# Weight loads issued by GpSimd, the second weight split in place, and the order planned anew

## The chip, the core and the metric

The kernel runs on one core of a Trainium2 chip. Its engines are TensorE (PE, with the weight load PEld beside it), VectorE (DVE), ScalarE (ACT), GpSimd (POOL) and SyncE (SP), which here only issues DMAs. Each engine works through its own queue in order, and semaphores tie the queues together. DMAs can be issued from SP, ACT and POOL. The metric is the device time in microseconds from launch to the last store; a profile of one execution stands beside the timed runs.

## The reference

Block-sparse attention feeds an MLP with the mish activation. The weights come as float64, everything else as float32.

```python
# attention: batch 4, heads 8, seq 768, head_dim 64, blocks of 32, 3 random blocks a row of blocks
scores = scale * np.matmul(q, k.transpose(0, 1, 3, 2))
mask = np.abs(blk_i - blk_j) <= 1            # the window
mask = mask | (blk_i == 0) | (blk_j == 0) | (blk_i == 23) | (blk_j == 23)   # the global blocks
...                                          # and the sampled blocks of each row
attn = softmax(np.where(mask, scores, -1e9))
x = (attn @ v).transpose(0, 2, 1, 3).reshape(3072, 512)
# MLP
h = x @ w_in                                 # 512 x 2048
g = h * np.tanh(softplus(h))
return (g @ w_out).astype(np.float32)        # 2048 x 512
```

## The kernel before

**Arithmetic.** Every matmul operand that must be exact is split in a high and a low float16 half, and three products (high-high, high-low, low-high) make one product. So each weight block goes through: a load of the float64 bits (1024 KB for one of the 8 blocks of w_in, 512 KB for one of the 16 of w_out), a decode to float32 on DVE in three integer operations (L873, L876, L879), a sum of squares on PE (the "gram", L361) from which a power-of-two scale comes, and the split in two halves. For w_in the split runs over PE (L947, L956) and casts on ACT or DVE (L951, L953). For w_out, `add_split` with `by_pe` false (`OPE` is 0) does it in three steps: scale the float32 into a temporary wt_o (ACT L963 or DVE L965), cast that to the high half (ACT L968 or DVE L969), and subtract on POOL to get the low half (L970). The decoded float32 block of w_out lies in the very bytes of wo that its two halves take later (`a0_o`).

**Attention.** The queries are worked on in jobs, 13 for each of four batches: first a dense one for the first global block, then pairs of query blocks, with the other dense one in between. A job makes the scores s (L661), their maximum (L703 to L708, DVE), the exponentials pt (L727, ACT), transposes t (L667, PE), the two halves ph (L750, ACT) and pl (L754, DVE; in the first three jobs PE L758 and ACT L763), the product with v (L789, into obank), the division (L808 to L811, DVE), a transpose tx and its halves xh (L836) and xl (L839). Keys of the random blocks are gathered by POOL copies (L598, or on ACT L595 in the first jobs), values by DMAs that SP issues (L615 to L622 for a pair, L637 for a dense job, L558 for the global blocks) from a copy vd in DRAM.

**MLP.** A tile is 256 tokens. Its h (L1049) comes in 8 parts; each pair of parts goes through scale (L1060), exponentials and logarithms (L1078 to L1086), L1087 and the halves g (L1094 or L1096, and POOL L1099); then y (L1114) takes four k steps for each half of the tile, which need the halves of w_out. The ring g has four places, so the h of the next tile can run ahead of the y of the tile before by no more than that.

**Order.** Nothing is scheduled by the compiler. Each step is a task with its engines, a duration in us and what it reads and writes. `Plan.emit` runs a model of the engines and, at each step, picks for the engine that is free first the task with the smallest sum of due time and key; the instructions are then written in that order. The keys stand in tables: `URGE` by kind of task, `JOBS` by job (the first 14), `PIECES` by weight block. `START` gives the earliest time at which PE may begin the scores of each of the first 14 jobs, and `pace` spreads the others. `fill` puts matmuls that do no work (L1309) into gaps of PE from 14 to 200 us. In the model a DMA takes its queue's time; it knows nothing of the semaphores that mark completion.

**Rings.** Buffers are handed out from rings of fixed length (`RINGS`). The ring "raw" has 6 places; it holds the loaded k, q and v of coming batches (L419), the v halves, the raw blocks of w_out, and the temporaries wt_o. The ring "wr" of raw w_in blocks has 3. `load_i` and `load_o` issue the weight loads, on ACT or, where the model finds it earlier (`BOTH`), on SP. All of them record line L865, in `load_w`.

The three steps of a w_out block before:

```python
nc.vector.tensor_scalar(out=t, in0=a0(), scalar1=sc(), scalar2=None, op0=ALU.mult)      # or ACT
nc.vector.tensor_copy(out=hi, in_=tl[kt])                                               # or ACT
nc.gpsimd.tensor_tensor(out=lo, in0=tl[kt], in1=hi, op=ALU.subtract)
```

Of the kernel before, what the change touches and what calls it, by code (L numbers as in the profile page):

```python
# [32 lines left out]
URGE = {"am": -30, "dgi": -29, "endsv": 24, "gh": 8, "gp": -3, "gram": 4, "gramv": 1, "hik": -7, "hiq": 20, "hiv": -7, "hs": 4, "hsw": -16, "k": -4, "kg": -1, "kw": -30, "mx": 19, "nb": -12, "o": 13, "p": -1, "ph": 2, "pl": -30, "q": 12, "r": 30, "rawk": 6, "rawq": 23, "rawv": 24, "s": -10, "sck": 12, "scq": -24, "scv": -3, "ssk": -22, "ssq": 1, "ssv": 9, "t": 14, "tpq": -30, "tpv": 2, "tpw": -12, "tx": -30, "us": -2, "v": -1, "vd": -9, "vg": 1, "wdi": -4, "whi": -3, "who": -30, "wli": -27, "wlo": -11, "wo": 19, "wor": 24, "wq": 7, "wr": -23, "ws": 1, "wto": 26, "xhw": 22, "xw": 10, "ys": -7}  # L33
JOBS = [-17, -8, 5, -19, 0, 1, -8, -9, -24, -11, 1, 1, -4, -26]
PIECES = [-4, -2, -1, 2, -1, 3, 5, 18, -23, -12, -10, -4, -3, -4, 3, 8, 7, 11, 13, 14, 16, 23, 31, 26]
# [29 lines left out]
class Plan:  # L65
# [4 lines left out]
    SEM = 0.06  # L70
# [53 lines left out]
    def emit(self, pace, fill):  # L124
# [6 lines left out]
        free, ready, dma, held = {}, {}, {}, {}  # L131

# [9 lines left out]
        while todo:  # L142
# [3 lines left out]
            for eng, ts in ready.items():  # L146
                f = free.get(eng, 0.0)
                cand = []
                for t in ts:
# [10 lines left out]
                    if len(t.ways) > 1:  # L160
                        done = {e: max(at, load.get(e, 0.0)) + x[0] for e, x in t.ways.items()}
                        if done[eng] > min(done.values()):
                            continue
                    start = self.port(held, eng, max(at, f), t.ways[eng][2])
# [17 lines left out]
            if t.kind and t.kind[0] == "dma":  # L182

                other = max([x for e, x in dma.items() if e != t.eng], default=0.0)
                at = max(dma.get(t.eng, 0.0), end)
                dma[t.eng] = at + t.kind[1] + min(t.kind[1], 0.5 * max(other - at, 0.0))
                t.end = max(dma[t.eng], end + t.lat)
# [21 lines left out]
def attn_mish_kernel(ctx: ExitStack, tc: tile.TileContext, qT, kT, v, sampled, blocks, w_in, w_out, out):  # L209
# [118 lines left out]
    BOTH = True  # L328
# [70 lines left out]
    def add_root(key, ss, fn, r, after, w, new, cls, n=1, apart=False, ring="t"):  # L399

        add("PE", 0.3 * n, lambda: root_pe(key, ss(), apart, ring), r=r, w=[key], new=[(ring, key)], key=cls - 2, lat=0.3)
        add("DVE", 0.6, fn, r=[key, *after], w=w, new=new, key=cls)

    def load(b, what, js, ring="raw", after=()):
# [3 lines left out]
        def fn():  # L408
# [15 lines left out]
            kind=("dma", 1.95 * n))  # L424
# [114 lines left out]
    def store_v(b, j):  # L539
        add("SP", 0.9, lambda: nc.sync.dma_start(  # L540
            out=vd[b][j * TT:(j + 1) * TT].rearrange("(c p) h d -> p c h d", p=P), in_=tl["v", b, j]),
            r=[("v", b, j)], w=[("vd", b, j)], key=-4, lat=2.5, kind=("dma", 2.0))
# [12 lines left out]
    def globals_v(b, n):  # L555
# [3 lines left out]
        add("SP", 0.9, fn, r=VD3(b), w=[("vg", n)], key=-1, lat=2.3, kind=("dma", 0.5))  # L559
# [46 lines left out]
    def gather_v(su):  # L606
# [6 lines left out]
        def fn():  # L613
# [10 lines left out]
            kind=("dma", 0.9))  # L624
# [733 lines left out]
```

## Time and profile before

| | |
|---|---|
| timed runs | 788.79, 789.8 and 790.77 us |
| median | 789.8 us |
| the profiled execution, first to last instruction | 786.6 us, mean granted clock 0.990 |
| h matmuls (L1049), PE busy | 282.8 + 209.8 us |
| y matmuls (L1114), PE busy | 278.0 us |
| weight loads: first and last issue of w_in | 10.5 and 50.9 us |
| weight loads: first and last issue of w_out | 60.4 and 105.3 us |
| first matmul of h, first of y | 102.6 and 143.0 us |
| bytes moved by DMA | 95.31 MB, on SP's queue 80.51 MB, on ACT's 12.85 MB |

The profiled execution's time is given as its span; 3.2 us lie between that and the median of the timed runs. Busy times of PE overlap, because matmuls are pipelined. A row of a group ends with the idle time of its engine just ahead of the group's instructions and with what ended it. A row of waits names who waited, for whom, how long in all, how often, and the longest. A row of a stage gives its length and the busy time of each engine in it. A row of a tile gives the shortest, the median and the longest duration in ns, and the first and last start.

### The profile page before, as it was taken

What the parts mean: (1) busy time and instruction counts of PE and PEld (TensorE: products, weight loads), DVE (VectorE), ACT (ScalarE), POOL (GpSimd) and SP (SyncE); (2) the same over time, 40 slices, a digit from 0 to 9 for tenths busy, and PEclk for the clock granted to TensorE, in tenths of its full rate; (3) what the DMA queues carried; (4) which work ended last, traced back from release to release, by engine and by line L of the source; (5) the groups of instructions that cost most, each with busy time, mean ns of one, the idle gap of its engine ahead of it and who ended that gap; (6) DMA issues with size and microseconds to landing.
All of it is one profiled execution on the core that took longest, in us unless ns stands there. A gap on an engine that the chain in (4) does not pass through costs nothing.

```text
span 786.6 us, 30628 instructions
## 1 busy us (share of the span) xinstructions
PE 740.5 (94%) x12793; PEld 518.7 (66%) x12793; DVE 493.5 (63%) x900; ACT 542.7 (69%) x880; POOL 307.6 (39%) x393
## 2 busy tenths in 40 slices
PE   6677899888999999999999999999999999999997
PEld 5544578665577767767776676677677667666663
DVE  6868988998767764795866457656665453223220
ACT  3555778768868877777887768786876666455650
POOL 2114244887635542374443422534641331213021
PEclk9989999999999999999999999999999999999999
DMA  9878857104534475244346603523444112000000
GB/s 339 263 236 256 268 176 202 44 2 136 159 117 131 119 198 171 69 162 120 87 139 194 192 15 101 174 77 91 119 115 119 37 39 81 14 15 14 14 14 27
DMA packets 57742, 95.31 MB, mean 121 GB/s; under 512 B 8323, under 2 KB 20612, under 8 KB 57604
## 3 DMA queue, kind: packets, MB, share of 16 engines
q1 hardware_dynamic: 52032, 80.51, 34.9%
q10 hardware_dynamic: 5572, 12.85, 4.8%
q8 instruction: 100, 1.64, 0.9%
q14 instruction: 38, 0.31, 0.1%
HBM read 80.38 MB, written 12.95 MB: 119 GB/s over the span
## 4 chain that ended last, share of the span: by engine, by line
PE 73%; DVE 10%; ACT 6%; DMA 5%; issue 2%; POOL 1%; SPq 1%; POOLq 1%; ACTq 0%; DVEq 0%
PE h_None L1049 27%; PE y L1114 26%; PE obank L789 6%; PE t L667 6%; PE s L661 4%; DMA vg<-vd 3%; PE tx L667 1%; PE wd_i L947 1%; DVE wt_o L965 1%; DMA wr<-in_moe_w_in_dram 1%; DVE hs_None L1087 1%; DVE v L491 1%; DMA raw_k<-in_k_dram 1%; ACT us_None L1078 1%; POOL kt L522 1%
## 5 line engine op out<-in xcount | busy, mean ns | idle before, releaser
L1049 PE MATMUL h_None<-xh,wi 128*128 128x256 f16 x1536 | 282.8, 273 | 0.0
L1114 PE MATMUL y<-wo,g 128*128 128x512 f16 x1152 | 278.0, 380 | 4.0 <-POOL wo L970 2.6
L1049 PEld LDWEIGHTS <-wi 128*128 128x128 f16 x2304 | 223.5, 98 | 47.3 <-issue 2.1
L1049 PE MATMUL h_None<-xl,wi 128*128 128x256 f16 x768 | 209.8, 273 | 0.0
L1114 PEld LDWEIGHTS <-g 128*128 128x128 f16 x1152 | 111.1, 98 | 106.7 <-issue 7.3
L1099 POOL TENSOR_TENSOR g<-hs_None,g 128x1024 f16<-128x1024 f32 x48 | 107.6, 2241 | 188.4 <-DVE g L1096 144.8
L598 POOL COPY kg<-kt 128x256 f16 x258 | 107.2, 451 | 123.3 <-PE s L661 109.7
L1060 ACT ACTIVATE hs_None<-h_None,gsc 128x512 f32<-128x512 f32 x96 | 65.5, 684 | 80.2 <-PE h_None L1049 79.4
L727 ACT ACTIVATE pt<-s,nb,ns 128x256 f32<-128x256 f32 (+1 forms) x208 | 106.3, 582 | 5.7 <-PE t L667 5.0
L750 ACT ACTIVATE ph<-t 128x512 f16<-128x512 f32 x112 | 66.5, 596 | 45.1 <-PE t L667 45.0
L754 DVE SCALAR_TENSOR_TENSOR pl<-t,ph 128x512 f16<-128x512 f32 x105 | 71.9, 686 | 35.8 <-ACT ph L750 35.5
L1087 DVE SCALAR_TENSOR_TENSOR hs_None<-us_None,hs_None 128x1024 f32<-128x1024 f32 x48 | 65.0, 1355 | 40.1 <-ACT us_None L1086 40.1
L667 PE MATMUL t<-ident,pt 128*128 128x128 f32 x448 | 70.4, 280 | 6.8 <-DVE pl L754 3.6
L708 DVE TENSOR_REDUCE mx<-s 128x4 f32<-128x1024 f32 x44 | 53.7, 1222 | 31.9 <-PE s L661 31.3
L1083 POOL TENSOR_TENSOR us_None<-us_None 128x1024 f32<-128x1024 f32 x22 | 44.2, 2007 | 71.8 <-DVE us_None L1081 68.7
L667 PEld LDWEIGHTS t<-ident,pt 128*128 128x128 f32 x448 | 51.6, 142 | 21.4 <-DVE pl L754 4.5
L789 PEld LDWEIGHTS <-ph 128*32 128x32 f16 x3584 | 47.9, 94 | 20.9 <-issue 13.1
L1078 ACT ACTIVATE us_None<-hs_None,hsc 128x1024 f32<-128x1024 f32 x48 | 55.2, 1150 | 0.9
L789 PE MATMUL obank<-vg,ph 128*32 128x65 f16 (+1 forms) x3200 | 50.6, 196 | 4.0 <-DMA vg<-vd 2.2
L1081 DVE TENSOR_SCALAR us_None<-us_None 128x1024 f32<-128x1024 f32 x48 | 37.4, 778 | 25.4 <-ACT us_None L1078 25.2
L1085 ACT ACTIVATE us_None<-us_None 128x1024 f32<-128x1024 f32 x48 | 50.7, 1056 | 1.6 <-POOL us_None L1083 0.8
L1086 ACT ACTIVATE us_None<-us_None 128x1024 f32<-128x1024 f32 x48 | 50.7, 1056 | 0.8
(199 smaller groups left out, 893.6 us busy)
## 6 DMA issues: line engine op xcount, KB each, us to landing
vg<-vd SPq DMA_DIRECT2D x320, 65.0 KB, 2.6
vg<-vd SPq DMA_DIRECT2D x80, 195.0 KB, 3.2
wr<-in_moe_w_in_dram ACTq DMA_DIRECT2D x8, 1024.0 KB, 7.4
vd<-v SPq DMA_DIRECT2D x12, 520.0 KB, 3.8
vg<-vd SPq DMA_DIRECT2D x12, 520.0 KB, 5.1
raw_k<-in_k_dram SPq DMA_DIRECT2D x12, 512.0 KB, 5.4
raw_q<-in_q_dram SPq DMA_DIRECT2D x12, 512.0 KB, 4.3
raw_v<-in_v_dram SPq DMA_DIRECT2D x12, 512.0 KB, 5.0
```

Of the source, the lines that this page charges most:

```text
L598: nc.gpsimd.tensor_copy(out=dst, in_=tl["kt", b][:, :, ds(j, BS)])
L667: nc.tensor.matmul(out, src, ident, start=start, stop=stop, is_transpose=True)
L727: ex = lambda o, x, g, w: nc.scalar.activation(out=o, in_=x, func=AF.Exp, bias=nb[:, g, w:w + 1], scale=tl["ns", b, sus[w]["qb"] // TB][:, ...
L750: nc.scalar.activation(out=new(sb, "ph", ("ph", i, j), [P, 2, 2, P], F16), in_=tl["t", i, j], func=AF.Copy, scale=PSC)
L754: nc.vector.scalar_tensor_tensor(out=new(sb, "pl", ("pl", i, j), [P, 2, 2, P], F16), in0=tl["t", i, j], scalar=PSC, in1=tl["ph", i, j], op ...
L789: nc.tensor.matmul(o[cs, w, g, 0:v1 - v0], p[:, k, g, cs], vt[:, k, 2 * c + g, v0:v1], start=j == 0 and g == 0 and k == 0 and n == 0, stop ...
L1049: nc.tensor.matmul(h[:, f2, 0:n].rearrange("p (s q) -> p s q", q=BS), wi[:, fp, cc // 2, w, cc % 2, fs], x[:, s0:s0 + sn, cc], start=f2 == ...
L1060: nc.scalar.activation(out=tl[kq][:, 2 * (fp % 2):2 * (fp % 2) + 2, 0:n], in_=tl[kh][:, :, 0:n], func=AF.Copy, scale=gsc[:, fp:fp + 1])
L1078: nc.scalar.activation(out=us(), in_=hs(), func=AF.Exp, scale=hsc[:, b:b + 1])
L1087: add("DVE", 1.32 * c, lambda: nc.vector.scalar_tensor_tensor(out=hs(), in0=us(), scalar=-0.5, in1=hs(), op0=ALU.add, op1=ALU.mult), r=[ku ...
L1099: add("POOL", 2.3 * c, lambda: nc.gpsimd.tensor_tensor(out=g(1), in0=hs(), in1=g(0), op=ALU.subtract), r=[kq, ("gh",) + kp], w=[kp], use=[kg])
L1114: nc.tensor.matmul(tl[ky], tl["g", b, t, k][:, g, f, q], wo[:, fc, w], start=fc == 0 and n == 0, stop=fc == NFC - 1 and n == 2)
```

## The change

The loads of both weights are issued by GpSimd alone, no longer by ACT or SP. A block of w_out is split in two operations and without a temporary: the high half is scaled straight out of the float32 block, on ACT or DVE, and DVE makes the low half in one operation (scale, then subtract the high half). The halves of block n are written where the float32 of block n - 2 was, which is free once that block's own halves are made; the halves of the first two go to a new buffer wx. In the planner, a DMA now takes the next of eight semaphores of its kind of queue (one set of eight for SP and ACT, one for POOL) and starts only when that semaphore's last DMA has landed; a task that issues several DMAs counts each, and the times of some are new. The first matmuls of h wait for the scale gsc in the plan, too, and the small matmul of a scale waits for what its DVE step waits for. The tables `URGE`, `JOBS`, `PIECES` and `START` have new numbers throughout; the earliest starts of the 14 first jobs are shown below.

```diff
...
-    SEM = 0.06
+    SEM, LANES = 0.06, 8
     def __init__(self, rings):
...
         free, ready, dma, held = {}, {}, {}, {}
+        lanes = {w: [[0.0] * self.LANES, 0] for w in ("hard", "soft")}
         def open_(t):
...
                             continue
+                    if t.kind and t.kind[0] == "dma":
+                        lane, n = lanes["soft" if eng == "POOL" else "hard"]
+                        at = max(at, lane[n % self.LANES])
                     start = self.port(held, eng, max(at, f), t.ways[eng][2])
...
             if t.kind and t.kind[0] == "dma":
-                other = max([x for e, x in dma.items() if e != t.eng], default=0.0)
-                at = max(dma.get(t.eng, 0.0), end)
-                dma[t.eng] = at + t.kind[1] + min(t.kind[1], 0.5 * max(other - at, 0.0))
-                t.end = max(dma[t.eng], end + t.lat)
+                lane, n, end, t.end = *lanes["soft" if t.eng == "POOL" else "hard"], start, 0.0
+                each = t.kind[1] / t.kind[2]
+                for k in range(n, n + t.kind[2]):
+                    end = max(end, lane[k % self.LANES]) + t.dur / t.kind[2]
+                    other = max([x for e, x in dma.items() if e != t.eng], default=0.0)
+                    at = max(dma.get(t.eng, 0.0), end + 0.3)
+                    dma[t.eng] = at + each + min(each, 0.5 * max(other - at, 0.0))
+                    lane[k % self.LANES] = land = max(dma[t.eng] + 0.5, end + t.lat + min(max(other - end, 0.0), 3.5))
+                    t.end = max(t.end, land)
+                lanes["soft" if t.eng == "POOL" else "hard"][1] += t.kind[2]
+                free[t.eng] = end
             else:
...
     NO, NZ = 4 * (D + 2), 240
-    BOTH = True
     pools = {"w": ctx.enter_context(tc.tile_pool(name="never", bufs=1))}
...
     def add_root(key, ss, fn, r, after, w, new, cls, n=1, apart=False, ring="t"):
-        add("PE", 0.3 * n, lambda: root_pe(key, ss(), apart, ring), r=r, w=[key], new=[(ring, key)], key=cls - 2, lat=0.3)
+        add("PE", 0.3 * n, lambda: root_pe(key, ss(), apart, ring), r=[*r, *after], w=[key], new=[(ring, key)], key=cls - 2, lat=0.3)
         add("DVE", 0.6, fn, r=[key, *after], w=w, new=new, key=cls)
...
             new=[(ring, key) for key in keys], key=-5 if b == 0 else 0, lat=2.0,
-            kind=("dma", 1.95 * n))
+            kind=("dma", 1.45 * n, n))
     def sums(b, what, j, cls):
...
             out=vd[b][j * TT:(j + 1) * TT].rearrange("(c p) h d -> p c h d", p=P), in_=tl["v", b, j]),
-            r=[("v", b, j)], w=[("vd", b, j)], key=-4, lat=2.5, kind=("dma", 2.0))
+            r=[("v", b, j)], w=[("vd", b, j)], key=-4, lat=2.5, kind=("dma", 2.0, 1))
     KT3 = lambda b: [("k", b, j) for j in T3]
...
                 nc.sync.dma_start(out=vgs[n][s * BS:(s + 1) * BS, 1], in_=vd[b][j * BS:(j + 1) * BS])
-        add("SP", 0.9, fn, r=VD3(b), w=[("vg", n)], key=-1, lat=2.3, kind=("dma", 0.5))
+        add("SP", 0.9, fn, r=VD3(b), w=[("vg", n)], key=-1, lat=2.3, kind=("dma", 0.5, 2))
     regs = {}
...
         add("SP", 2.9, fn, r=VD3(b) + ["off", "z"] + [("reg", k) for k, _ in slots(su)], w=[("vg", n)], key=-3, lat=2.4,
-            kind=("dma", 0.9))
+            kind=("dma", 1.5, 2 + NR - 1 + (w0 - qb != -1 or w1 - qb != 2)))
     def fetch_dense(su):
...
                 w=[("vg", j) if j < NVG else ("vt", b)], new=[("raw", ("vt", b))] if j >= NVG else (),
-                key=-3, lat=2.4, kind=("dma", 2.0))
+                key=-3, lat=2.4, kind=("dma", 2.0, 1))
...
             go = lambda eng: load_w(pools["w"], raw, "wr", src, None, eng)
-            add("ACT", 0.45, lambda: go(nc.scalar), r=after, w=[raw], new=[("wr", raw)], key=-9, lat=2.0,
-                kind=("dma", 3.9), also=[("SP", 0.5, lambda: go(nc.sync), False)] if BOTH else ())
+            add("POOL", 1.0, lambda: go(nc.gpsimd), r=after, w=[raw], new=[("wr", raw)], key=-9, lat=2.0,
+                kind=("dma", 3.9, 1))
             return
-        add("ACT", 0.45, lambda: load_w(None, None, None, src, a0_i(k).rearrange("p (c f) -> p c f", c=NCC),
-                                          nc.scalar), r=after,
-            w=[key], key=-9, lat=2.0, kind=("dma", 1.95))
+        add("POOL", 1.0, lambda: load_w(None, None, None, src, a0_i(k).rearrange("p (c f) -> p c f", c=NCC),
+                                        nc.gpsimd), r=after,
+            w=[key], key=-9, lat=2.0, kind=("dma", 1.95, 1))
     def piece_i(k, cls):
...
             also=[("DVE", 0.68, lambda: cast("DVE", lo), False)])
+    SH = 2
+
+    def wo_at(fc):
+
+        return pools["wx"][:, fc] if fc < SH else wo[:, fc - SH]
+
     def a0_o(fc):
         go = lambda eng: load_w(sb, raw, "raw", w_out.rearrange("(c p) f -> p c f", p=P)[:, fc], a0_o(fc), eng)
-        add("ACT", 0.45, lambda: go(nc.scalar), r=after, w=[raw] + ([] if wide else [("wo", fc)]), new=[("raw", raw)],
-            key=-5, lat=2.0, kind=("dma", 1.95), also=[("SP", 0.5, lambda: go(nc.sync), False)] if BOTH else ())
+        add("POOL", 1.0, lambda: go(nc.gpsimd), r=after, w=[raw] + ([] if wide else [("wo", fc)]), new=[("raw", raw)],
+            key=-5, lat=2.0, kind=("dma", 1.95, 1))
     def piece_o(fc, cls):
...
     def parts_o(fc, cls):
-        if fc == 0:
-            add_diag(("o",), lambda: sc_o, "sc_o", cls)
-        add_split(("o", fc), ("o",), lambda: a0_o(fc), wo[:, fc, 0], wo[:, fc, 1], ("wo", fc), RINGO, cls,
-                  lambda: sc_o, "sc_o", fc % 4 < OPE)
+
+        before = [(w, "o", fc - SH) for w in ("wh", "wl")] if fc >= SH else ["open"]
+        kh, kl = ("wh", "o", fc), ("wl", "o", fc)
+
+        def hi(eng):
+            if eng == "ACT":
+                nc.scalar.activation(out=wo_at(fc)[:, 0], in_=a0_o(fc), func=AF.Copy, scale=sc_o)
+            else:
+                nc.vector.tensor_scalar(out=wo_at(fc)[:, 0], in0=a0_o(fc), scalar1=sc_o, scalar2=None, op0=ALU.mult)
+        add("ACT", 0.62, lambda: hi("ACT"), r=[("wo", fc), "sc_o", *before], w=[kh], key=cls,
+            also=[("DVE", 0.45, lambda: hi("DVE"), True)])
+        add("DVE", 0.72, lambda: nc.vector.scalar_tensor_tensor(
+            out=wo_at(fc)[:, 1], in0=a0_o(fc), scalar=sc_o, in1=wo_at(fc)[:, 0], op0=ALU.mult, op1=ALU.subtract),
+            port=True, r=[("wo", fc), "sc_o", kh], w=[kl], key=cls)
     def scales_w():
...
         for f2 in range(2):
-            mlp(1.31 if part is None else 0.85, lambda f2=f2: fn(f2), r=[*PARTS_I(fp), *xs], w=[kh, "h in order"],
+            mlp(1.31 if part is None else 0.85, lambda f2=f2: fn(f2), r=[*PARTS_I(fp), "gsc", *xs], w=[kh, "h in order"],
                 new=[("h", kh)] if f2 == 0 else (), use=[("xh", b, t), ("xl", b, t)])
...
                 for n, (g, w) in enumerate(((0, 0), (0, 1), (1, 0))):
-                    nc.tensor.matmul(tl[ky], tl["g", b, t, k][:, g, f, q], wo[:, fc, w],
+                    nc.tensor.matmul(tl[ky], tl["g", b, t, k][:, g, f, q], wo_at(fc)[:, w],
                                      start=fc == 0 and n == 0, stop=fc == NFC - 1 and n == 2)
...
                 also=[("ACT", 0.7, lambda: ys_fn("ACT"), False)])
-            add("SP", 0.4, out_fn, r=[kys], lat=2.0, kind=("dma", 1.1))
+            add("SP", 0.4, out_fn, r=[kys], lat=2.0, kind=("dma", 1.1, 1))
...
         pools["m"] = pools["cm"].__enter__()
+        pools["wx"] = pools["m"].tile([P, SH, 2, DM], F16, name="wx", tag="wx", bufs=1)
     LPE = 4
-    OPE = 0
-    RINGO = "t"
     AT0, ATV, ATW = -19.0, -13.0, -4.0
...
     add("ACT", 1.0, lambda: which(new), w=["off", "z"],
-        new=[("hs", ("z",))], key=-9, lat=6.0)
+        new=[("hs", ("z",))], key=-9, lat=6.0, kind=("dma", 0.9, 2 + B))
     for j in T3:
...
     total = sum(t.ways["PE"][0] for t in plan.tasks if t.kind and t.kind[0] == "M")
-    RES, START = 595.0, [0, 58, 39, 56, 33, 120, 63, 62, 76, 58, 107, 143, 72, 148]
+    RES, START = 595.0, [9, 54, 61, 56, 37, 142, 59, 75, 33, 90, 112, 155, 52, 144]
     at = {"done": 0.0, "next": 0.0, "job": 0, "last": None, "shape": None, "open": False}
...
```

`add_decode`, the gram and the split of w_in stay as they are.

More of the change, by code (lines that the diff above doesn't have):

```diff
@@ L28 @@
              wq=2, am=2, dg=2)
-URGE = {"am": -30, "dgi": -29, "endsv": 24, "gh": 8, "gp": -3, "gram": 4, "gramv": 1, "hik": -7, "hiq": 20, "hiv": -7, "hs": 4, "hsw": -16, "k": -4, "kg": -1, "kw": -30, "mx": 19, "nb": -12, "o": 13, "p": -1, "ph": 2, "pl": -30, "q": 12, "r": 30, "rawk": 6, "rawq": 23, "rawv": 24, "s": -10, "sck": 12, "scq": -24, "scv": -3, "ssk": -22, "ssq": 1, "ssv": 9, "t": 14, "tpq": -30, "tpv": 2, "tpw": -12, "tx": -30, "us": -2, "v": -1, "vd": -9, "vg": 1, "wdi": -4, "whi": -3, "who": -30, "wli": -27, "wlo": -11, "wo": 19, "wor": 24, "wq": 7, "wr": -23, "ws": 1, "wto": 26, "xhw": 22, "xw": 10, "ys": -7}
-JOBS = [-17, -8, 5, -19, 0, 1, -8, -9, -24, -11, 1, 1, -4, -26]
-PIECES = [-4, -2, -1, 2, -1, 3, 5, 18, -23, -12, -10, -4, -3, -4, 3, 8, 7, 11, 13, 14, 16, 23, 31, 26]
+URGE = {"am": -11, "dgi": -30, "endsv": 30, "gh": 14, "gp": -24, "gram": 30, "gramk": 30, "gramq": 1, "gramv": -6, "hik": -26, "hiq": -2, "hiv": -22, "hs": -2, "hsw": -7, "k": 23, "kg": 5, "kw": -22, "mx": 28, "nb": -7, "o": 14, "p": 1, "ph": -15, "pl": -20, "q": 3, "r": 30, "rawk": -24, "rawq": 2, "rawv": 30, "s": -9, "sck": 30, "scq": -26, "scv": -6, "ssk": -9, "ssq": 2, "ssv": 2, "t": 29, "tpk": 14, "tpq": -27, "tpv": -6, "tpw": -22, "tx": -20, "us": -5, "v": -30, "vd": -21, "vg": 29, "wdi": 4, "whi": 5, "who": -13, "wli": -21, "wlo": -16, "wo": 19, "wor": 30, "wq": 8, "wr": -24, "wto": 26, "xhw": 16, "xw": -12, "ys": 4}
+JOBS = [-30, -22, 0, -1, 30, 10, -17, -30, -30, -28, -9, 1, -11, -30]
+PIECES = [-3, 0, -6, 2, -1, 14, 20, 30, -6, -26, -8, -2, 5, -19, 16, 5, 9, 17, 11, 13, 1, 12, 29, 30]
 def place(w):
```

## The prediction

> **What bounds the kernel now.** I read the page's head first, then the busy time by stage, then the waits of the two bad stages, and last the tiles that the change touches.
>
> ```profile
> span 786.6 us, 30628 instructions
> PE 740.5 (94%) x12793; PEld 518.7 (66%) x12793; DVE 493.5 (63%) x900; ACT 542.7 (69%) x880; POOL 307.6 (39%) x393
> 0.00:40.00 40.00, 26.55 (x481) 21.88 (x482) 30.38 (x78) 18.24 (x28) 8.15 (x23) 1.00 0.87 298
> 40.00:100.00 60.00, 47.74 (x1077) 29.10 (x1075) 47.51 (x99) 38.83 (x84) 16.37 (x27) 0.91 0.83 257
> 100.00:140.00 40.00, 38.74 (x1044) 32.78 (x1044) 33.69 (x69) 33.31 (x63) 19.32 (x27) 1.00 0.63 180
> 140.00:180.00 40.00, 32.24 (x396) 23.35 (x381) 39.01 (x50) 28.44 (x41) 33.22 (x26) 1.00 0.05 15
> 180.00:200.00 20.00, 20.00 (x293) 12.57 (x292) 16.00 (x27) 17.41 (x31) 15.42 (x18) 0.91 0.53 160
> 200.00:600.00 400.00, 393.91 (x7808) 280.54 (x7807) 268.54 (x498) 307.86 (x518) 176.23 (x251) 1.00 0.44 126
> 600.00:700.00 100.00, 99.52 (x1217) 68.40 (x1216) 39.71 (x62) 58.61 (x81) 21.26 (x15) 1.00 0.17 49
> 700.00:786.60 86.60, 81.79 (x515) 50.09 (x513) 18.70 (x22) 39.98 (x43) 17.66 (x8) 0.99 0.05 19
> ```
>
> The columns of the stages are the length, then the busy time of PE, its weight load, DVE, ACT and POOL, then the granted clock, the DMA share and GB/s. TensorE bounds the kernel from 200 us on: it idles 6.1 us of 400, then 0.5 and 4.8. Before 200 us it idles 13.5, 12.3, 1.3 and 7.8 us (length less busy), and some of its busy time is no work: the filler of L1309.
>
> ```profile
> 0.00:40.00 40.00, 11.23 (x88) 9.18 (x89) 1.00 0.87 298
> 40.00:100.00 60.00, 4.33 (x24) 1.96 (x21) 0.91 0.83 257
> ```
>
> So 15.6 us are filler. The clock of 0.91 costs about 47.74 x 0.09 = 4.3 us in 40:100 and 20.0 x 0.09 = 1.8 us in 180:200. Together, idle 46.1, filler 15.6 and clock 6.1 make 68 us that are not work at full clock. Nothing in the diff changes the matmul work, so a gain can only come out of these 68 us, and nearly all of what the changed operations touch lies before 200 us: 21 us in 40:100 and 9.6 us in 140:200.
>
> In 140:180 DVE is the bound (39.01 of 40) and the DMA engines stand still (share 0.05). Why they do, the waits and the timeline of SP's own queue tell:
>
> ```profile
> SPq L419 <- POOL wo L970: 22.9, 3, 20.3
> SPq L419 <- ACT wo L968: 19.0, 1, 19.0
> 132.41 8.24 SPq L637 DMA_DIRECT2D vg<-vd  x3
> 179.96 3.77 SPq L419 DMA_DIRECT2D raw_v<-in_v_dram  x3
> ```
>
> L419 loads v of the second batch into the ring "raw". It waits 42 us for slots that the temporary wt_o of the second weight's split holds. SP issues in order, so nothing leaves it from 140.65 to 179.96 us.
>
> In 40:100 the largest hole is this, from the waits of the first 100 us and the timeline:
>
> ```profile
> ACT wi L951 <- DMA vg<-vd: 6.4, 1, 6.4
> PE wd_i L956 <- ACT wi L951: 5.5, 1, 5.5
> 48.68 0.38 ACTq L865 DMA_DIRECT2D wr<-in_moe_w_in_dram  x1
> ```
>
> ACT's next compute reads nothing of vg. What waited was the weight load at 48.68, which stands ahead of it in ACT's queue, and it was released by the landing of one of SP's gathers. The two share their completion semaphores; that is how I read it. PE stood 5.5 us behind it.
>
> **The change, part by part.**
>
> 1. *24 weight loads go to POOL.* Eight of w_in leave ACT, sixteen of w_out leave ACT and SP, eight each.
>
> ```profile
> L865 ACTq DMA_DIRECT2D wr<-in_moe_w_in_dram x8: 374/374/520, 10.5 to 50.9; - x8
> L865 ACTq DMA_DIRECT2D wor<-in_moe_w_out_dram x8: 334/366/710, 60.4 to 89.3; - x8
> L865 SPq DMA_DIRECT2D wor<-in_moe_w_out_dram x8: 328/362/852, 82.8 to 105.3; - x8
> SPq L865 <- DVE wo L879: 5.0, 3, 2.2
> ```
>
> ACT is rid of 16 x 0.37 = 6 us of issuing, SP of 8 x 0.36 = 2.9 us and of the 5.0 us in which its gathers stood behind a w_out load that had no free slot. The hole of 5.5 us on PE goes, since POOL's loads count on semaphores of their own. What is late next there is DVE, 47.51 busy of 60, which decodes both weights. So I take 3.5 us of the 5.5, and 2 of the 4.3 us of clock, which is lowest right behind the hole: -5.5. Ends: 0 (DVE ends last all the same) and -9.8 (all of both).
>
> POOL pays. No row of before shows a load issued there. The nearest from below is the same load on ACT, 0.37 us; from above, the longest ordinary operation on POOL:
>
> ```profile
> L1099 POOL TENSOR_TENSOR g<-hs_None,g 128x1024 f16<-128x1024 f32 x48 | 107.6, 2241 | 188.4 <-DVE g L1096 144.8
> L598 POOL COPY kg<-kt 128x256 f16 x258 | 107.2, 451 | 123.3 <-PE s L661 109.7
> ```
>
> 24 loads are 9 to 54 us of POOL. It is busy 8.15 + 16.37 + 19.32 = 44 us of the first 140, so 96 are free; the plan itself charges 1.0 us for one, 24 us in all, and I take that. What it can delay are the key gathers (L598) queued behind a load that waits for its slot; they make s, which PE needs. The 5.0 us that SP waited so would now be POOL's, and I let 1 us of it reach PE: +1, ends 0 and +5. A gain from this queue below nothing is not seen: the loads keep their sizes and the same DMA engines, at a share of 0.83.
>
> 2. *The split of w_out.* Each of 16 blocks had three steps: scale into wt_o, cast the high half, subtract on POOL. It gets two: the high half scaled straight out of the float32 (ACT or DVE), the low half on DVE in one operation.
>
> ```profile
> L970 POOL TENSOR_TENSOR wo<-wt_o,wo x16: 1155/1328/2137, 140.1 to 181.8; 128x512 f16<-128x512 f32 x16
> L965 DVE TENSOR_SCALAR wt_o<-wo,cols x13: 470/639/2353, 138.6 to 177.9; 128x512 f32<-128x512 f32 x13
> L969 DVE CAST wo<-wt_o x12: 411/416/1258, 139.6 to 181.1; 128x512 f16<-128x512 f32 x12
> L963 ACT ACTIVATE wt_o<-wo,cols x3: 709/712/722, 154.8 to 180.3; 128x512 f32<-128x512 f32 x3
> L879 DVE SCALAR_TENSOR_TENSOR wo<-wor,wo x16: 674/685/1203, 67.1 to 130.1; 128x512 int32<-128x512 int32 x16
> L965 DVE TENSOR_SCALAR wt_o<-wo,cols 128x512 f32<-128x512 f32 x13 | 11.6, 907 | 0.0
> L969 DVE CAST wo<-wt_o 128x512 f16<-128x512 f32 x12 | 6.6, 565 | 0.4 <-ACT wt_o L963 0.4
> L970 POOL TENSOR_TENSOR wo<-wt_o,wo 128x512 f16<-128x512 f32 x16 | 22.6, 1421 | 7.7 <-DVE wo L969 6.4 <-DVE tp_k L394 1.0 <-ACT wo L968 0.3
> ```
>
> DVE loses 11.6 + 6.6 = 18.2 us. It gets 16 low halves; the row nearest is L879, the same kind of operation with both inputs in SBUF, 0.685 us: 11.0 us. With half of the high halves at 0.47 it is 14.8 us. POOL loses 22.6 us. The larger part is what DVE wins elsewhere, because operations beside POOL's subtractions run longer:
>
> ```profile
> L1087 DVE SCALAR_TENSOR_TENSOR hs_None<-us_None,hs_None x48: 1207/1225/3144, 127.0 to 765.7; 128x1024 f32<-128x1024 f32 x48
> 138.00:184.00 46.00, 9.24 (x4) 0.96 0.11 32
> L1081 DVE TENSOR_SCALAR us_None<-us_None x48: 675/693/2627, 116.3 to 761.6; 128x1024 f32<-128x1024 f32 x48
> 138.00:184.00 46.00, 6.47 (x4) 0.96 0.11 32
> ```
>
> Four of L1087 took 9.24 us in 138:184 against 4 x 1.225, four of L1081 6.47 against 4 x 0.693: 8.0 us too much. DVE is freed of 18.2 - 14.8 + 8.0 = 11 us of the 39. The chain by slots (block n writes where n-2 was) needs about eight rounds of 0.47 + 0.685, 9 us, under the 14.8, so it doesn't bind. The split took 43 us; the loads that now leave SP 40 us earlier no longer wait for it. PE lost 7.8 + 1.8 us in 140:200. I take 6 of the 9.6, since the attention chain through DVE and ACT stays: -6, ends 0 and -9.6. The chain that ended last runs through DVE wt_o, hs and us there, which is why I don't take less.
>
> 3. *The order.* The planner now knows eight semaphores for each kind of queue; the first matmuls of the MLP wait for gsc, and all keys and the earliest starts of the first 14 jobs are new (job 5 at 142 where it was 120). No row prices an order. From both sides: it can give back the 12.3 - 5.5 = 6.8 us of idle time left in 40:100, and lose as much. I take 0. The 13.5 us and 11.2 us of filler before 40 us are the first loads and scales, and stay.
>
> **Sum:** -5.5 + 1 - 6 + 0 = -10.5 us. The span would be 776. The profile gives 786.6 between the first and last instruction; the median of the runs is 789.8, 3.2 us more, for what lies around. I carry that over: 779.3, said as 779.
>
> **The rivals.**
>
> *More than that.* If the order also fills the 6.8 us and the ends -9.8 and -9.6 are met, the sum is -26: 764. For it: DMA stands idle 40 us now, so much can move. Against: DVE stays near its limit up to 130 us with the decode. I give 775 to 764 a chance of 0.24.
>
> *Nothing.* PE's holes close, and another wait opens at the same place (DVE's decode in 40:100, ACT's chain in 140:180), with the +5 of POOL: 787 to 792. Chance 0.08. That the loads leave ACT and SP is plain from the diff; that the hole at 44 us belongs to the shared semaphores is not.
>
> *Slower: POOL can't keep the pace of the w_out loads.* The sixteen went out between 60.4 and 105.3, one in 3.0 us. POOL works 27% of 40:100 (16.37 of 60), so 2.2 us of each 3.0 are free. Above 2.2 us a load, issue and waiting together, the last one is late. If a load costs 0.37 plus a DVE operation it must wait out (1.22 us, the longest of the decode) plus one on POOL ahead of it (2.24), that is 3.8 us, sixteen take 16 x 3.8 / 0.73 = 83 us where they had 48, and y of the first tile comes 35 us later, while PE has only the next tile's h and attention to do. A third to a half of that on PE is +12 to +17, less the 6 of the split: 796 to 801. Chance 0.2.
>
> The Trainium skill speaks for this one ("SBUF — State Buffer", section "SBUF: two separate sides"): a DMA issued from GpSimd has its descriptors written by GpSimd, which is locked out while VectorE runs an operation that holds both port pairs; its advice is to issue from ACT or SP. The page gives 620 ns alone and about 3100 beside such copies; by that, 2.5 us more for each of 24 loads is an estimate of 60 us of POOL. No run here has a load from POOL, but that DVE and POOL block each other agrees with L1087's 3.1 us.
>
> **How the numbers follow.** The forecast, 775 to 787, has 0.48; more 0.24; nothing 0.08; slower 0.2. Two in ten may be left out: the outermost of the "more" case below 764 and of the slow case above 797. Range 764 to 797. A measurement can tell 0.3%, 2.4 us, from no change. Faster by that (below 787.4): 0.72; within: 0.08; slower: 0.2.
>
> **What would show it.** Right: no wait of L419 on the split of wo; DMA share above 0.3 in 140:180; DVE's L1087 near 1.23 there; no hole of 5 us on PE near 45 us; PE idle before 200 us down from 35 to about 25. Wrong: idle time of PE before L661 or L947 put down to POOL or to a weight load; w_out loads landing later than 111 us; the matmuls of y starting later than 143 us; new idle time after 200 us, which would be the order's.

## The result and the profile after

The changed kernel takes 798.57 us (median of 4, 796.47 to 800.99) where the kernel before took 789.29 (788.59 to 790.77) beside it: a ratio of 1.0124, with a 95% interval of 1.0096 to 1.0153. It is 9.3 us slower; the prediction said 10.5 us faster, and 798.57 lies outside its range. The profiled execution has a span of 797.7 us, 11.1 more than before.

The head of the page and the busy time by stage, in the columns of the table of before (length, busy PE, weight load, DVE, ACT, POOL, granted clock, DMA share, GB/s), and below them the filler alone (now L1334) in the first two stages:

```profile
span 797.7 us, 30619 instructions
PE 743.7 (93%) x12792; PEld 520.6 (65%) x12792; DVE 505.5 (63%) x905; ACT 549.9 (69%) x882; POOL 294.0 (37%) x393
0.00:40.00 40.00, 22.83 (x356) 18.48 (x356) 24.98 (x58) 17.02 (x26) 9.86 (x23) 1.00 0.69 249
40.00:100.00 60.00, 46.32 (x1166) 29.84 (x1168) 49.03 (x107) 39.95 (x84) 28.37 (x44) 0.92 0.90 250
100.00:140.00 40.00, 36.48 (x1005) 27.78 (x982) 34.51 (x60) 29.25 (x57) 16.95 (x31) 0.99 0.67 199
140.00:180.00 40.00, 37.21 (x586) 29.78 (x585) 36.80 (x61) 33.94 (x51) 20.64 (x16) 1.00 0.41 121
180.00:200.00 20.00, 18.71 (x345) 12.42 (x344) 19.75 (x31) 18.18 (x30) 9.36 (x6) 1.00 0.20 62
200.00:600.00 400.00, 388.66 (x7464) 274.92 (x7463) 272.02 (x497) 308.51 (x509) 170.54 (x254) 0.99 0.43 122
```

```profile
0.00:40.00 40.00, 9.68 (x76) 1.00 0.69 249
40.00:100.00 60.00, 4.48 (x25) 0.92 0.90 250
```

Read it against before, stage by stage. PE idles 17.2 us in the first 40 (13.5 before), 13.7 in 40:100 (12.3), 3.5 in 100:140 (1.3), 2.8 and 1.3 in 140:200 (7.8 and 0), and 11.3 in 200:600 (6.1). So the stage of the split did get better, as forecast, and the others got worse: the start and the time behind 200 us most, 100:140 and 40:100 a little. Over the whole span PE idles 54.0 us where it idled 46.1, and the other 3.2 of the 11.1 us are longer busy time. The change is not one effect but several of both signs.

The start shows itself in the waits of PE in the first 20 us of after, and in one row of the timeline of POOL's queue:

```profile
PE gram_k L371 <- DMA raw_k<-in_k_dram: 5.9, 3, 5.0
PE gram_q L371 <- DMA raw_q<-in_q_dram: 4.4, 1, 4.4
PE gram_v L371 <- DMA raw_v<-in_v_dram: 3.0, 1, 3.0
2.37 2.49 POOL L875 DMA_DIRECT2D wr<-in_moe_w_in_dram  x3
```

The last two waits are new in this stretch: q and v come later. The first three loads of w_in, 1024 KB each, leave POOL at 2.37 us, ahead of v, which SP issues from 5.0 us. Before, they left later. Rows of the timelines of DVE and ACT before:

```profile
10.27 0.15 DVE L396 TENSOR_SCALAR sc_k<-tp_k 128x1 int32<-128x1 int32 x1
...
10.45 1.15 ACT L487 ACTIVATE kt<-raw_k,sc_k 128x1024 f16<-128x1024 f32 x1 [8.41 <-DMA raw_v<-in_v_dram]
10.46 1.53 ACTq L865 DMA_DIRECT2D wr<-in_moe_w_in_dram  x3
```

In ACT's queue the three loads stood behind kt, which reads the scale sc_k that DVE ends at 10.42, and in the program each of them carries a wait for an earlier DMA besides (of zeros into vd, of q), since SP's and ACT's DMAs share their completion semaphores. Nothing in the program says that w_in shall come after v; its place in the queue of an engine that had to wait for the scale had the effect. POOL had nothing ahead of them. The price is in the landing times of the first batch's v (shortest, median, longest), before and after:

```profile
DMA to landing us min/median/max: 5.6/5.9/6.1
```

```profile
DMA to landing us min/median/max: 13.6/13.8/14.0
```

### The profile page after: what moved, and what is told of

Its sections match the earlier page's. It is cut to its first block, busy times and chain, and to the rows that moved or that the text cites. A ratio compares the mean times of both kernels' runs of the same rounds, so it can differ in the third digit from the quotient of the medians.

```text
span 797.7 us, 30619 instructions
## 1 busy us (share of the span) xinstructions
PE 743.7 (93%) x12792; PEld 520.6 (65%) x12792; DVE 505.5 (63%) x905; ACT 549.9 (69%) x882; POOL 294.0 (37%) x393
## 4 chain that ended last, share of the span: by engine, by line
PE 72%; DMA 8%; DVE 8%; issue 3%; POOL 3%; ACT 2%; SPq 2%; POOLq 1%; DVEq 0%; ACTq 0%
PE y L1140 28%; PE h_None L1075 26%; PE t L677 5%; PE obank L799 5%; PE s L671 5%; DMA vg<-vd 4%; DMA raw_v<-in_v_dram 2%; DMA wor<-in_moe_w_out_dram 2%; DVE wo L1032 1%; PE tx L677 1%; SPq L577 1%; DVE v L501 1%; POOL kg L608 1%; POOL kt L532 1%; DVE wo L889 1%
## 5 line engine op out<-in xcount | busy, mean ns | idle before, releaser
L1140 PE MATMUL y<-wo,g 128*128 128x512 f16 x1008 | 245.4, 382 | 0.0
L608 POOL COPY kg<-kt 128x256 f16 x255 | 110.0, 466 | 130.7 <-PE s L671 120.6
L1113 DVE SCALAR_TENSOR_TENSOR hs_None<-us_None,hs_None 128x1024 f32<-128x1024 f32 x48 | 67.4, 1405 | 33.4 <-ACT us_None L1112 33.3
L677 PEld LDWEIGHTS t<-ident,pt 128*128 128x128 f32 x448 | 51.8, 143 | 13.7 <-issue 2.6
L1109 POOL TENSOR_TENSOR us_None<-us_None 128x1024 f32<-128x1024 f32 x17 | 34.6, 2036 | 57.5 <-DVE us_None L1107 56.5
```

Of the source, the lines that this page charges most:

```text
L608: nc.gpsimd.tensor_copy(out=dst, in_=tl["kt", b][:, :, ds(j, BS)])
L677: nc.tensor.matmul(out, src, ident, start=start, stop=stop, is_transpose=True)
L1113: add("DVE", 1.32 * c, lambda: nc.vector.scalar_tensor_tensor(out=hs(), in0=us(), scalar=-0.5, in1=hs(), op0=ALU.add, op1=ALU.mult), r=[ku ...
L1140: nc.tensor.matmul(tl[ky], tl["g", b, t, k][:, g, f, q], wo_at(fc)[:, w], start=fc == 0 and n == 0, stop=fc == NFC - 1 and n == 2)
```

## The experiments

Eighteen kernels ran; each group was timed beside the kernel before on its own chip, and ratios are to that. "Same order" means that every queue keeps the instructions of before, but for the edit.

**Where the loads are issued.** The loads alone on POOL, same order (b_pool), and the same with the first three held back (b_pool_hold): a copy of one column of v's second part into their buffer makes them wait until that part has landed.

```diff
-        eng.dma_start(out=raw.rearrange(
+        nc.gpsimd.dma_start(out=raw.rearrange(
# b_pool_hold besides, ahead of the load:
+        key[0] == "wr" and key[1] < 3 and nc.gpsimd.tensor_copy(out=raw[:, 0:1].bitcast(F32), in_=tl["flat", "v", 0, 1][:, 0:1])
```

> The kernel before, its order untouched, but each weight load is issued by POOL at the place in the program where ACT or SP issued it. Theory 1 (collision at the start: three loads of w_in leave at 2.4 us, ahead of v, because nothing makes them wait any more; v lands some 7 us later and all behind it): 794 to 798, gram of v near 18 us. Theory 2 (a load costs more from POOL all the way through: issue, descriptors, queue): 794 to 800, with each w_in load landing 3 us later throughout. Theory 3 (the new order and keys are the loss): 788 to 790, no change.

> As the run before, and the first three loads of w_in are held until the second load of v has landed, by a copy of one column on POOL ahead of each. Theory 1: back to 788 to 791. Theory 2: stays at 794 to 800. Theory 3: 788 to 790.

b_pool: 794.46 us, 1.0108 [1.0045, 1.0170]. b_pool_hold: 790.49 us, 1.0047 [1.0017, 1.0076]. So POOL's queue alone, with neither the new split nor the new order, is slower, and about half of it goes when the three loads wait for v: the two intervals overlap, but eight of the ten runs of b_pool_hold are faster than all four of b_pool. Rows of the loads, of the copy and of the landing of v in b_pool_hold:

```profile
L865 POOL DMA_DIRECT2D wr<-in_moe_w_in_dram x8: 748/751/962, 12.7 to 56.4; - x8
L864 POOL COPY wr<-raw_v x3: 187/482/1321, 12.2 to 15.2; 128x1 f32<-128x1 f32 x3
DMA to landing us min/median/max: 5.3/5.6/5.9
```

v lands as fast as before again. That a load is slower from POOL all the way through, the rival I had named, isn't seen: those of w_in land after 10.1 us in the median in b_pool, but after 7.8 in b_pool_hold and 7.4 before, the first two by these rows:

```profile
DMA to landing us min/median/max: 7.0/10.1/15.0
DMA to landing us min/median/max: 6.0/7.8/9.8
```

But the last w_in load now leaves at 56.4 us where it left at 50.9: POOL waits 13.7 us in four of these loads for a free slot, and its key gathers stand behind.

The same two edits on the changed kernel: its loads issued by ACT in the new order (a_act), and its first three loads held on POOL (a_hold).

```diff
# a_act
-        eng.dma_start(out=raw.rearrange(
+        nc.scalar.dma_start(out=raw.rearrange(
# a_hold: the copy of b_pool_hold ahead of the load
```

> The changed kernel, its order untouched, but every weight load is issued by ACT again, at its place in the program. Theory 1: the loads wait for the semaphores they share with SP, so the start recovers: 790 to 794 (ACT's own stalls may cost 2 or 3 us of it). Theory 2: 788 to 792. Theory 3: 796 to 800, no change.

> The changed kernel with the first three loads of w_in held until the second load of v has landed. Theory 1: 789 to 793, first h matmul near 104 us instead of 113, first filler at 14 us. Theory 2: 796 to 800. Theory 3: 796 to 800.

a_act: 793.13 us, 1.0079 [1.0046, 1.0111]. a_hold: 791.16 us, 1.0063 [1.0034, 1.0093]. Both are better than the change's 1.0124 (a_act's interval overlaps the change's a little), and neither is level: POOL isn't all of it. The first matmul of h comes at 107.8 us in a_hold, 112.9 in after; I had expected 104. In a_act no load is issued by POOL, and yet:

```profile
L875 ACTq DMA_DIRECT2D wor<-in_moe_w_out_dram x16: 334/334/814, 64.3 to 127.3; - x16
```

The late loads of w_out (before, the last left at 105.3) come from the order in which the queues were written and not from POOL's pace.

**The split alone, and only part of the loads.** b_split has the new split of w_out and nothing else: loads on ACT and SP, old planner, old tables, same order up to the split. b_pool_o has the sixteen w_out loads on POOL, same order. b_split_pool_o has both.

```diff
# b_split: parts_o and wo_at of after, and its buffer
+        pools["wx"] = pools["m"].tile([P, SH, 2, DM], F16, name="wx", tag="wx", bufs=1)
# b_pool_o
-        eng.dma_start(out=raw.rearrange(
+        (nc.gpsimd if key[0] == "wor" else eng).dma_start(out=raw.rearrange(
```

> The kernel before with the second part of the change alone: w_out split in two operations without the temporary, loads still on ACT and SP, the old planner and the old tables. Every queue runs as before up to the split at 138 us. My prediction put 6 us on this part (ends 0 and 9.6): by it 776 to 786, and 780 in the middle, with no wait of SP's loads of v on the split, and PE idle less in 138:200. Rival: the 40 us in which SP stood cost PE nothing, because nothing that it would have loaded was needed by then: 785 to 787, with the same PE idle time.

> The kernel before, same order, with only the sixteen loads of w_out issued by POOL; w_in stays where it was. With all loads on POOL and the first three held back the time was 0.5% over before. If POOL's queue is slow for the w_out loads, or key gathers stand behind them, that 0.5% is seen here: 789 to 791. If what was left came from the w_in loads (the later of them waiting in POOL's queue, h starting 2.6 us late), this gives 785 to 787. If the 5 us hole on PE near 45 us goes with the w_out loads gone from ACT, below 784; I hold that unlikely, because the load behind which ACT stood there was one of w_in.

> Both of the two edits above in one kernel: the new split, and w_out loaded by POOL, old planner and tables. If they touch different stretches (loads 60 to 110 us, split after 138 us), their differences add up within 1.5 us. If the time that the split gains hangs on when the loads of w_out came, they don't.

b_split: 780.26 us, 0.9918 [0.9882, 0.9954]. b_pool_o: 788.70 us, 1.0027 [1.0004, 1.0051]. b_split_pool_o: 781.03 us, 0.9941 [0.9918, 0.9965]. The split is worth 0.8%, w_out on POOL costs about a quarter of a per cent, with the split and without (with it, the intervals overlap). Three stages of b_split, then two rows of SP's waits between 100 and 200 us, then four of the operation that was L1087 (here L1103) in 138:184:

```profile
140.00:180.00 40.00, 40.00 (x628) 30.01 (x613) 35.85 (x61) 36.80 (x57) 24.19 (x18) 1.00 0.19 64
180.00:200.00 20.00, 19.69 (x298) 12.28 (x297) 13.17 (x25) 15.12 (x24) 14.41 (x20) 1.00 0.53 157
200.00:300.00 100.00, 99.12 (x2154) 72.21 (x2152) 69.42 (x142) 80.92 (x144) 42.60 (x68) 1.00 0.51 150
```

```profile
SPq L419 <- DVE q L491: 22.5, 1, 22.5
SPq L1148 <- DVE ys L1144: 13.0, 1, 13.0
```

```profile
138.00:184.00 46.00, 4.98 (x4) 1.00 0.22 71
```

PE idles 0.3 us in 140:200 (7.8 before), and four of L1103 take 4.98 us (9.24 before). The two longest of PE's waits in 138:200 before, which b_split no longer has, were on DVE and on the split itself, and none there was on a DMA:

```profile
PE t L667 <- DVE pl L754: 3.6, 1, 3.6
PE y L1114 <- POOL wo L970: 2.6, 3, 0.9
```

So what paid in this stage is the time of the engines that do the split, and of DVE beside them. SP's queue moves too: the first load of the next v leaves at 140.7 us instead of 179.96, though SP then stands 22.5 and 13 us for other things and the DMA share is only 0.19. What these earlier loads are worth behind 200 us, no run here separates.

**The hole on ACT, and whether the parts add.** b_split_late is b_split with the last five w_in loads on POOL, the first three on ACT as before; one of these five stood ahead of the 5.5 us hole of PE. b_split_pool is b_split with all 24 loads on POOL.

```diff
# b_split_late
+        (nc.gpsimd if key[0] == "wr" and key[1] > 2 else eng).dma_start(out=raw.rearrange(
# b_split_pool
+        nc.gpsimd.dma_start(out=raw.rearrange(
```

> The kernel before with the new split, same order, and the last five of the eight w_in loads on POOL; the first three stay on ACT, behind the loads of k, q and v, and w_out stays on ACT and SP. My prediction took 3.5 us (with the clock 5.5) for the hole of 5.5 us on PE that one of these late loads causes on ACT. By it, 3.5 to 5.5 us less than the new split alone (0.9918 of before): ratio 0.985 to 0.988, first matmul of h near 99 us. Rival: the hole closes and the time goes into the next wait (the attention chain, or the late loads waiting in POOL's queue): ratio 0.990 to 0.995, first h at 102 to 104.

> The kernel before with the new split and all 24 loads on POOL, in the old order: the two parts of the change without the new planner and tables. If the parts add, the ratio is 0.992 for the split times 1.011 for the loads, 1.003 (789 us), and the rest of the change's 1.012, about 1 per cent, belongs to the new order. If the split cannot pay once the start is late, it is 1.008 to 1.012, and the order costs nothing.

b_split_late: 779.51 us, 0.9873 [0.9814, 0.9931]; b_split_pool: 788.20 us, 0.9995 [0.9966, 1.0023]. The product of the two parts, 0.9918 x 1.0108 = 1.0025, lies just above b_split_pool's interval; with the errors of the two factors, the parts add. For b_split_late the ratio lies where my price for the hole had put it, but its interval overlaps that of b_split, its span is 777.8 to 777.0, and its first matmul of h at 102.4 to 101.7, as the rival said; a gain isn't shown. What became of the hole is seen in stages from 40 us of one execution each, first of b_split, then of b_split_late:

```profile
40.00:50.00 10.00, 4.53 (x114) 2.89 (x114) 5.19 (x5) 2.27 (x6) 3.07 (x6) 0.96 0.77 208
50.00:60.00 10.00, 9.94 (x141) 5.57 (x140) 5.92 (x9) 7.09 (x18) 0.00 (x0) 0.70 0.75 248
60.00:80.00 20.00, 15.82 (x454) 10.21 (x454) 17.20 (x40) 13.51 (x32) 8.37 (x13) 1.00 0.81 264
```

```profile
40.00:50.00 10.00, 9.85 (x132) 5.96 (x130) 7.18 (x8) 6.21 (x15) 4.34 (x8) 0.81 0.83 256
50.00:60.00 10.00, 7.92 (x243) 6.88 (x242) 7.70 (x17) 6.52 (x13) 2.05 (x3) 0.83 1.05 257
60.00:80.00 20.00, 15.89 (x367) 10.10 (x355) 14.57 (x32) 11.99 (x29) 7.33 (x13) 0.83 0.79 243
```

The hole closes (9.85 of 10 busy instead of 4.53), and the time goes elsewhere: 2 us of it into the next stage's idle time, and the granted clock is lower in the first stage and the third (0.81 and 0.83 where it was 0.96 and 1.00; in the second, 0.83 for 0.70).

**The order.** Level with before with both parts in the old order (0.9995), 1.0124 in the new: 1.2 to 1.3% are left for the planner and its tables. b_split_model has the new split, loads on ACT and SP, the planner of after (without the two edits around gsc) and the old tables. a_oldmodel has the new split, the loads as tasks of POOL, and the planner and tables of before. a_oldkeys is the kernel after with the four tables of before; a_oldmodel_newkeys is a_oldmodel with the tables of after.

```diff
# b_split_model: lanes in emit and the new DMA times, with the tables of before
# a_oldkeys: URGE, JOBS, PIECES and START of before in the kernel after
# a_oldmodel: emit and DMA times of before, no edit around gsc, tables of before, and
+            add("POOL", 1.0, lambda: go(nc.gpsimd), r=after, w=[raw], new=[("wr", raw)], key=-9, lat=2.0,
```

> The kernel after, with the four tables (URGE, JOBS, PIECES, START) of before; planner with semaphores, loads on POOL and the new split stay. Theory 3 (the new tables lose the time): about 790 or less, since it would then be before plus the collision at the start less the split. The other theory (the new tables are matched to the new model, and the loss is the collision of the first loads): no faster than after, 797 to 815, with the first matmul of h at 110 us or later.

> The new split, loads on ACT and SP as before, and the new planner (eight semaphores for each kind of queue, the new times of DMAs) with the old tables. Theory A, the order that the new model makes is the worse one on the chip, whatever loads the weights: ratio 1.000 to 1.010, that is 6 to 14 us over the new split alone, with PE's matmuls of h starting after 105 us or PE idle by 5 us more in 200:300. Theory B, the order of the new model is as good and only the loads on POOL spoil it: 0.990 to 0.995.

> The new split and the loads as tasks of POOL in the plan, with the old planner and the old tables; so the planner is free to issue the loads as early as it likes on POOL. Theory A (the new model's order is the loss): like the new split with all loads on POOL in the old order, or within 0.4 per cent of it. Theory B (planning the loads on POOL is the loss): near 1.012 like the change itself.

> Loads as tasks of POOL, the new split, the old planner and the new tables: the fourth corner beside old planner with old tables (0.9998 of before), new planner with old tables (1.0121) and the change itself (1.0124). If the planner's model is the loss and the tables are neutral: 0.998 to 1.003. If the new tables also lose when they stand alone: 1.008 to 1.03. If they win and the model hides it: below 0.995.

| loads on POOL, new split | old tables | new tables |
|---|---|---|
| old planner | 0.9998 [0.9968, 1.0027] | 1.0162 [1.0130, 1.0194] |
| new planner | 1.0121 [1.0082, 1.0161] | 1.0124 [1.0096, 1.0153] |

b_split_model, with the loads on ACT and SP, is at 1.0371 [1.0315, 1.0426], far beyond what either theory had said. Whoever leaves the old pair of planner and tables loses 1.2% or more, and the new pair doesn't win it back. The two stages in which a_oldmodel and after differ most, 40:100 and 200:300, of a_oldmodel and the second of after; then the largest wait of PE in 40:100 and in 200:300 in after, and the same wait in 40:100 in a_oldmodel:

```profile
40.00:100.00 60.00, 52.24 (x1232) 33.32 (x1230) 46.52 (x103) 41.80 (x91) 28.98 (x49) 0.91 0.84 245
200.00:300.00 100.00, 99.03 (x2087) 70.04 (x2086) 68.09 (x134) 78.73 (x141) 50.99 (x70) 1.00 0.54 152
```

```profile
200.00:300.00 100.00, 92.01 (x1875) 63.45 (x1874) 73.25 (x131) 74.18 (x130) 48.91 (x77) 0.97 0.49 141
```

```profile
PE obank L799 <- DMA vg<-vd: 4.8, 3, 2.7
PE obank L799 <- DMA vg<-vd: 3.9, 2, 2.5
PE obank L788 <- DMA vg<-vd: 1.4, 2, 0.8
```

PE idles 7.8 us in 40:100 with the old planner, 13.7 in after; 1.0 in 200:300, and 8.0 in after. In after PE waits for gathered values (vg), 4.8 us in 40:100 and 3.9 in 200:300; in a_oldmodel for these 1.4 and 0.5. So in the new order late gathers are the largest single wait in both stages. They aren't the whole loss: a_nogsc, below, has no such wait in 200:300 and is as slow as after. Why they come late isn't shown.

Five more runs looked for the piece of the order that does it, and for the price of the start in a third order: after without the eight semaphores in the model (a_nolanes), after without the two edits around gsc (a_nogsc), after with the old START (a_start), a_oldmodel with the new START (a_oldmodel_start), and a_oldmodel with the first three loads held (a_oldmodel_hold).

```diff
# a_nolanes
-    SEM, LANES = 0.06, 8
+    SEM, LANES = 0.06, 1000
# a_nogsc
-        ... r=[*PARTS_I(fp), "gsc", *xs] ...      r=[*r, *after]
+        ... r=[*PARTS_I(fp), *xs] ...             r=r
# a_start (and, the other way, a_oldmodel_start)
-    RES, START = 595.0, [9, 54, 61, 56, 37, 142, 59, 75, 33, 90, 112, 155, 52, 144]
+    RES, START = 595.0, [0, 58, 39, 56, 33, 120, 63, 62, 76, 58, 107, 143, 72, 148]
```

> The kernel after with 1000 semaphores for each kind of queue in the planner's model instead of eight: the new times of DMAs, the new tables and all else stay. If the eight semaphores in the model are what makes the order worse: 1.000 to 1.005. If the new DMA times, the tables or the wait of h for gsc are it, nothing moves: 1.009 to 1.016. Tables made for another model may cost more: above 1.016.

> The kernel after without two small edits of the planner: the first matmuls of h no longer wait for gsc in the plan, and the small matmul of a scale does not wait for what its DVE step waits for. If they hold the first matmul of h back (112.9 us in after, 100.8 us with the old planner): first h before 107 us and a ratio of 1.002 to 1.007. If not: 1.009 to 1.016 and first h at 110 to 114 us.

> The kernel after with the earliest job starts (START) of before, where job 5 may begin at 120 us instead of 142 and job 11 at 143 instead of 155; the other tables, the planner, the loads and the split stay new. If the late starts make the idle 10.8 us (8.0 and 2.8 of clock) of PE in 200:300: that falls to 2 to 4 us and the ratio to 1.003 to 1.008. If it is the new URGE, JOBS and PIECES or the model: 1.010 to 1.016, with 6 us or more still idle there.

> Loads as tasks of POOL, the new split, old planner and old tables, but the new START alone (without it the ratio was 0.9998, with all new tables 1.0162). If START carries the loss of the tables: 1.010 to 1.018. If the other three tables carry it: 0.998 to 1.004. Between these, both carry a part.

> Loads as tasks of POOL, the new split, the old planner and the old tables, and the first three w_in loads held back until the second part of v has landed (one column of it is copied into their buffers first). Without the hold this was 0.9998 of before. If the collision of these loads with k, q and v costs 0.6 per cent in this order as it did in the two others: 0.993 to 0.995. If its first h, at 100.8 us already, is not bound by the start: 0.998 to 1.001.

a_nolanes: 1.0144 [1.0084, 1.0203]; a_nogsc: 1.0139 [1.0098, 1.0180]. Neither the eight semaphores nor the waits for gsc carry the loss; the planner's new DMA times weren't run alone. a_start: 1.0227 [1.0201, 1.0254], worse than the change; a_oldmodel_start: 1.0520 [1.0489, 1.0551]. Each START does worse among the other set of tables, so a table can't be priced by itself: a miss for both of my readings there. a_oldmodel_hold: 783.98 us, 0.9960 [0.9934, 0.9986], 0.4% under a_oldmodel and between the two ranges that I had given; its first h comes at 93.6 us instead of 100.8. By the medians, holding the first loads paid in all three orders, 0.6, 0.6 and 0.4%, though in the first and the third of these pairs the intervals overlap.

Four kernels here have intervals wholly below before: b_split (0.8% faster), b_split_late (1.3%), b_split_pool_o (0.6%) and a_oldmodel_hold (0.4%). All have the new split and the old planner and tables, and none lets the first three loads leave ahead of v. The runs can't tell b_split and b_split_late from each other.

## Why the prediction was wrong

**Part 1, the loads leave ACT and SP: -5.5.** The mechanism was right, and the price stays open. The hole near 45 us is gone from after, and b_split_late, which closed it alone, shows that the late w_in loads on ACT made it; but its gain over b_split is not shown (0.9873 and 0.9918 with overlapping intervals). I had taken 2 us of better clock as a gain; the profile of b_split_late shows a lower clock in 40:50 and 60:80 instead, beside fuller use of PE in the first.

**Part 1, the cost on POOL: +1.** This step failed. I priced POOL's time, and that was, if anything, too high; rows of after:

```profile
L875 POOL DMA_DIRECT2D wr<-in_moe_w_in_dram x8: 748/786/1208, 2.4 to 55.6; - x8
L875 POOL DMA_DIRECT2D wor<-in_moe_w_out_dram x16: 528/528/838, 56.5 to 131.3; - x16
```

An issue takes 0.79 or 0.53 us, not the 1.0 of the plan. What I didn't price is when the first loads go. My sentence "The 13.5 us and 11.2 us of filler before 40 us are the first loads and scales, and stay" was wrong: idle time there is 17.2 us. I had the 10.5 us of the first issue in a quoted row, and never asked what held it until then. In the old order the loads on POOL cost 1.08%, some 8.5 us, where I had +1 - 5.5 us. Some 0.6% is the start (b_pool against b_pool_hold), a quarter of a per cent the w_out loads (b_pool_o). The rest is left to the other w_in loads, by subtraction only; the waits for slots in POOL's queue fit it.

**Part 2, the split: -6.** Right in sign and size: -0.82% in b_split, 6.1 us between its median and that of before (9.6 between the spans). The rows of after stand beside the estimates:

```profile
L1032 DVE SCALAR_TENSOR_TENSOR wo<-wo,cols x14: 739/750/1834, 169.8 to 190.2; 128x512 f16<-128x512 f32 x14
L1029 DVE TENSOR_SCALAR wo<-wo,cols x5: 472/480/616, 171.3 to 189.7; 128x512 f16<-128x512 f32 x5
L1027 ACT ACTIVATE wo<-wo,cols x9: 707/715/723, 166.4 to 184.5; 128x512 f16<-128x512 f32 x9
```

0.750 us for a low half (estimate 0.685), 0.48 for a high half on DVE (0.47), and only 5 of 16 of those on DVE instead of half. The 8 us that L1087 and L1081 lost beside the old split were the larger part, as I had it: in b_split four of L1087 fell from 9.24 to 4.98 us, four of L1081 from 6.47 to 2.71. That loads "leave SP 40 us earlier" came true in b_split, for the first of v (140.7 us); what it is worth isn't shown. In after the gain is there too (4.1 us idle in 140:200 for 7.8, and no loss of clock), but behind 200 us, in 200:300, PE idles 5.2 us more than before.

**Part 3, the order: 0, ends of 6.8 us either way.** This step failed as well, and it is half of the miss. Parts 1 and 2 together, -10.5 in my sum, came out level in the old order (0.9995), and from there to 1.0124 the order costs 1.3%, some 10 us. My ends came from the idle time left in 40:100 alone, and a new order acts on the whole kernel: 5.2 us of idle time are new in 200:600. Part of it is waits for gathered values; which piece of planner or tables does it stays open.

**The rivals.** The slower one gave 796 to 801, and 798.57 lies in it by luck, since its reason isn't what happened. POOL kept the pace: in b_pool_o the sixteen loads go out from 63.2 to 104.9 us (60.4 to 105.3 before) and its first y starts at 142.5. A late y is no disaster either: in a_oldmodel the last w_out load leaves at 133.6 us, y starts at 164.5, and the time is level with before. The Trainium skill ("SBUF — State Buffer", section "SBUF: two separate sides") gives about 3100 ns for a DMA issued from GpSimd beside a copy on VectorE, where it takes 620 alone. In after the longest issue takes 1.21 us and the median 0.79 or 0.53, with DVE busy 49 of 60 us in 40:100, and in b_pool_o the w_out loads land after 7.1 us in the median where before has 6.2. A delay of 2.5 us a load isn't seen; how many of VectorE's operations here hold both port pairs, no view tells.

**The signs I had named.** No wait of SP on the split of wo: true. DMA share above 0.3 in 140:180: true (0.41), and no sign of anything, since b_split has 0.19 and is the faster. No 5 us hole near 45: true. L1087 near 1.23 us in 138:184: 1.41 in after, 1.25 in b_split. Idle time before 200 us down to 25: false, 38.5. Three of the four warning signs came: w_out loads to 131.3 us, y at 165.2, new idle time after 200 us. But a_act has the first two with no load on POOL (127.3 and 161.5), and a_oldmodel has them without a price. The fourth, PE waiting for POOL or a weight load ahead of L661 or L947, doesn't show in the first 200 us.

## What to carry to other kernels

Before moving a DMA to another queue, ask what held it where it was: the instructions ahead of it and the waits that it carried may have been the only thing that kept it behind more urgent loads. If so, write that order down as a dependency. Price a hole by what is late next, the clock included, and give a newly planned order a wide error of its own: here the two parts in the old order came out level, and the new order alone decided the sign.

## What was not expected of the hardware

Three 1024 KB loads issued at 2.37 us more than doubled the landing time of 512 KB loads on another queue issued from 5.0 us, from 5.9 to 13.8 us (5.6 where they were held back, in b_pool_hold). An issue on POOL takes 0.75 to 0.88 us in the median for a 1024 KB load of w_in and 0.53 us for a 512 KB one of w_out, where ACT takes 0.37 for both.
